# Linformer attention and a squared-ReLU FFN on one core: softmax sums of a whole batch in the free half of a PSUM pair, and the first batch's v ahead of the weights

## The chip, the core and the metric

The kernel runs on one core of a Trainium2 chip. The metric is device time in microseconds (us), lower is better. The core has TensorE (PE; its weight loads are shown as PEld), VectorE (DVE), ScalarE (ACT), GpSimd (POOL) and SyncE (SP). Transfers are issued from a queue of SP (plain copies and transposes) or of POOL (here all loads that turn float32 into bfloat16) and are carried out by 16 DMA engines. Matmul results go to PSUM, which has eight banks of 512 float32 per partition.

## What is computed

```python
k_proj = einsum('ks,bhsd->bhkd', E, k)          # B = 8, H = 8, S = 1024, D = 64; 64 projected keys
v_proj = einsum('ks,bhsd->bhkd', F, v)
scores = q @ k_proj.T / sqrt(D)
attn = exp(scores - max); attn = attn / (sum(attn) + 1e-9)
x = (attn @ v_proj) as (B*S, H*D)               # 8192 x 512
out = relu(x @ w_in) ** 2 @ w_out               # 512 -> 2048 -> 512
```

Inputs and output are float32; the kernel works in bfloat16 with float32 sums.

## The kernel before, in words

**Tiling.** A batch is 1024 tokens, cut into two chunks of 512 (`Chunk`). Attention of a batch (`Attention`) works on head pairs: `project` makes k and v projections of all heads with 16 matmuls into the two banks of one PSUM pair (k into rows 0 to 63 of bank 0, v into rows 64 to 127 of bank 1; the other halves of both banks are unused, L267 to L274). A DMA transpose makes `kT` from `kp` (L304), another makes `qT` from `Q_sb` (L331). `scores(pr)` multiplies them for one head pair (L363) and ScalarE takes the exponential into `expT`. `sums_spread(pr)` (L387) sums the exponentials of two head pairs with eight matmuls against a block of ones, each into 32 rows; ScalarE inverts the sums as exp(-ln) over 128 x 1024 (L397, L398), and eight copies on SP's queue spread them over the partitions as `rs` (L404). `values(pr)` (L407) multiplies the exponentials with v, and VectorE multiplies the result with `rs` into `xT` (L420).

**FFN.** Both layers use Strassen's seven products instead of eight, with pre-made sums of the weights (`w_in_sum`, `w_out_sum`), of `xT` (`sum_x`) and of `h` (`sum_h`). `Group` makes the first layer (L666), `second_spread` the second (L586). Batch 0 is an exception: its first layer runs as plain 512-column matmuls (`first_cold`, `first_plain`, L503), and `second_seven` (L563) does the second layer of its first chunk.

**Order.** TensorE's order is written out by hand. After the start, the generator `both()` (L863) takes one step after the other; a step is four matmuls of a first-layer product and four of a second-layer product, and a batch has 56 steps. `at` and `on` hang stages of attention on step numbers in `plan` (L753, L869), so that attention of the coming batches runs between the FFN products of earlier ones. The loop at L876 does so with t = 56 (b - 1) + 28. All other engines, and the queues of SP and POOL, are ordered by the framework's scheduler, which places each instruction by its own estimate of when its inputs are there; the order is fixed in the program, and each queue runs strictly in it.

**Buffers around the change.** From L824 on one PSUM pair serves all of attention (`att_psum`, L75), so each stage waits for the reader of the one before. `K_sb`, `Q_sb`, `V_sb`, `kp`, `kT` and `qT` have one buffer each, `vp` two, `expT` four, `rs` three, the output tile `o_sb` three. A load of the next `Q_sb` must wait until the DMA transpose has read the old one. `load_kv` and `load_q` are given a `behind` (L91): the load waits for a named instruction.

**Start of the run.** Transfers are issued in the order k (two heads as float32 on SP), k, q, F, k, q, v heads 0 to 3, then w_in piece 0, v heads 4 and 5, w_in piece 1, v heads 6 and 7, more w_in, the rest of q, and w_out (L102 to L146). `warm(n)` (L218) puts n matmuls on zeros between early stages. v's second half is projected in two pieces at steps 1 and 2 of `first_cold` (L778, L780), and `chunk_values` for heads 4 to 7 follows in two halves (L779, L781).

Of the kernel before, what the change touches and what calls it, by code (L numbers as in the profile page):

```python
# [9 lines left out]
P = 128  # L10
# [9 lines left out]
def kernel(  # L20
# [19 lines left out]
    NI = 8  # L40
# [61 lines left out]
    e_f32 = soft_pool.tile([KP, S], F32, tag="rs", name="e_f32")  # L102
    nc.sync.dma_start(e_f32[:], E[:])

    k_f32 = soft_pool.tile([P, 2, NI, D], F32, tag="rs", name="k_f32")
# [13 lines left out]
    V_PIECES = (slice(0, 4), slice(4, 6), slice(6, 8))  # L119
    load(V0[:, V_PIECES[0]], tokens(v, 0, h=V_PIECES[0]))  # L120
# [7 lines left out]
    W_IN_PIECES = ((0, 2), (2, 4), (4, 8), (8, 12), (12, 16))  # L128
# [100 lines left out]
    nc.vector.memset(kp[:], 0.0)  # L229
    kT = const_pool.tile([P, H, 2, KP], BF16, name="kT")  # L230
    VALUE_QUADS = ((LO, 0, 0, LO), (HI, 1, 1, HI), (HI, 0, 1, LO), (LO, 1, 0, HI))

    class Attention:
# [97 lines left out]
        def transpose_q_dma(self):  # L331
            nc.sync.dma_start_transpose(
                self.qT[:].rearrange("p h n t -> p (h n) t"), self.Q[:].rearrange("p h i d -> p (h i d)")
            )
# [22 lines left out]
        def inverse(self, ps):  # L357
            rs = soft_pool.tile([P, 2, TCH], F32, tag="rs", name="rs")
# [9 lines left out]
        def sums(self, pr):  # L368
# [8 lines left out]
            rs = [soft_pool.tile([P, 2, TCH], F32, tag="rs", name="rs") for _ in range(2)]  # L377
# [9 lines left out]
        def sums_spread(self, pr):  # L387

            ps = att_psum()
            for j in range(2):  # L390
                for o, par, a, r in VALUE_QUADS:
                    c = 32 * (2 * a + j)
                    nc.tensor.matmul(  # L393
                        ps[c:c + 32, par], lhsT=ones[r, 0:32], rhs=self.e[pr + j][r, a], start=True, stop=True
                    )
            inv = soft_pool.tile([P, 2, TCH], F32, tag="rs", name="inv")
            nc.scalar.activation(inv[:], ps[:], AF.Ln)  # L397
            nc.scalar.activation(inv[:], inv[:], AF.Exp, scale=-1.0)  # L398
            for j in range(2):
                rs = soft_pool.tile([P, 2, TCH], F32, tag="rs", name="rs")  # L400
                for a in range(2):
                    have = 32 * (2 * a + j)
                    for to in (64 * a, 64 * a + 32):
                        nc.sync.dma_start(rs[to:to + 32], inv[have:have + 32])  # L404
                self.rs[pr + j] = rs
# [316 lines left out]
    with tc.manual_schedule(engines={PE}):  # L722
# [152 lines left out]
        on(15, 1, "chunk_values", 1, 1)  # L875
        for b in range(B - 1):  # L876
            t = 56 * (b - 1) + 28
            if b:
                on(t + 1, b + 1, "scores", 3)
                on(t + 3, b + 1, "sums_spread", 2)  # L880
                on(t + 7, b + 1, "values", 0)
                on(t + 10, b + 1, "values", 1)
                on(t + 20, b + 1, "values", 2)
                on(t + 23, b + 1, "values", 3)
                at(t + 24, lambda b=b: chunk[b + 1, 0].sum_x())
            at(t + 51, lambda b=b: chunk[b + 1, 1].sum_x())
            if b + 2 < B:
                if b:
                    on(t + 11, b + 2, "load_q", lambda b=b: atts[b + 1].done)
                on(t + (26 if b else 32), b + 2, "transpose_q_dma")  # L890
                on(t + (28 if b else 36), b + 2, "project")
                on(t + (30 if b else 37), b + 2, "transpose_k_dma")
                if b + 3 < B:
                    at(t + (32 if b else 37), begin, b + 3)
                    on(t + (32 if b else 37), b + 3, "load_kv", lambda b=b: atts[b + 2].kT_done)
                on(t + (44 if b else 45), b + 2, "scores", 0)
                on(t + (47 if b else 48), b + 2, "scores", 1)
                on(t + (50 if b else 51), b + 2, "sums_spread", 0)
                on(t + (53 if b else 54), b + 2, "scores", 2)
# [34 lines left out]
```

## Time and profile before

| | |
|---|---|
| time, median of 3 runs | 475.4 us (475.11 to 475.48) |
| the profiled execution, its own time | 475.91 us, of which the span is 474.1 us |
| TensorE matmuls | 464.5 us, 98% of the span, 4136 instructions |
| VectorE | 348.1 us, 73% |
| ScalarE | 296.5 us, 63% |
| POOL | 34.3 us, 7% |
| granted TensorE clock | 1.0 |
| first-layer products L666, second-layer products L586 | 37.0% and 35.6% of the chain that ended last |
| Ln and Exp of the sums, L397 and L398 | 12 each, 1023 and 1062 ns |
| spreads `rs<-inv`, L404 | 96 on SP, 128 KB each, 2.3 us to landing (median) |
| loads of Q, K, V after the start | 1024 KB each as landed, medians 12.4, 10.2 and 14.8 us to landing |

How to read it: the span is the profiled time from the first to the last instruction. The "chain that ended last" follows the last instruction back through what released each step. A line of a timeline has start, duration, engine, line, operation, output and input, shapes and count; in brackets the idle time of that engine ahead of it and what ended it. Durations of single matmuls are modelled with their drain, so the step from one start to the next tells more than the duration. "To landing" is the time from the issue of a transfer to its completion.

### The profile page before, as it was taken

Reading aid. Unit: us, or ns where it says so; the run is one execution under the profiler, and the core shown is the slowest. Engines: PE = TensorE matmul, PEld = TensorE weight load, DVE = VectorE, ACT = ScalarE, POOL = GpSimd, SP = SyncE. Lnnn points to the kernel's source line nnn. Section 1 sums busy time; section 2 is a strip of 40 time slices with the busy share of each in tenths; the row PEclk is TensorE's granted clock in tenths of the full one; section 3 lists DMA queues with packets and bytes.
Section 4 is the critical chain, followed back from the end, with each engine's and each line's share of the span. In section 5 each row is a group of like instructions: output and inputs, shape, how many; then the busy total and the mean of one; then the engine's idle time right before and its main releaser. Section 6 shows DMA issues by size and latency. Waiting matters only on the chain.

```text
span 474.1 us, 10128 instructions
## 1 busy us (share of the span) xinstructions
PE 464.5 (98%) x4136; PEld 367.6 (78%) x4154; DVE 348.1 (73%) x593; ACT 296.5 (63%) x482; POOL 34.3 (7%) x47
## 2 busy tenths in 40 slices
PE   7899999999999999999999999999999999999996
PEld 3444587787888887887878888888878888888885
DVE  2468976776977779677895679777796778968571
ACT  2478676777556873687556775568736875565641
POOL 7430010100010000100001000100000000000000
PEclk9999999999999999999999999999999999999999
DMA  9999999795879568795987948796592054101012
GB/s 177 203 205 207 154 169 189 160 225 140 160 167 195 158 104 185 129 193 132 181 180 122 190 113 145 181 190 163 105 218 81 29 134 107 66 24 68 24 68 88
DMA packets 85231, 67.90 MB, mean 143 GB/s; under 512 B 34368, under 2 KB 81728, under 8 KB 85184
## 3 DMA queue, kind: packets, MB, share of 16 engines
q0 software_dynamic: 31696, 29.23, 40.3%
q1 hardware_dynamic: 53344, 37.89, 30.4%
q8 instruction: 32, 0.52, 0.4%
q10 hardware_dynamic: 144, 0.13, 0.1%
q14 instruction: 15, 0.12, 0.1%
HBM read 59.24 MB, written 16.78 MB: 160 GB/s over the span
## 4 chain that ended last, share of the span: by engine, by line
PE 93%; ACT 2%; DMA 2%; DVE 2%; issue 1%; ACTq 0%; DVEq 0%; POOLq 0%
PE ps_bank L666 37%; PE ps_second L586 36%; PE ps_bank L503 4%; PE ps_bank L563 3%; PE ps_att L271 3%; PE ps_att L340 2%; PE ps_second L563 2%; PE ps_att L416 2%; DMA K_sb<-in_k_dram 1%; PE ps_bank L315 1%; DVE xT L445 1%; PE ps_att L393 1%; DMA out_dram<-o_sb 1%; ACT h L496 1%; PE ps_att L350 0%
## 5 line engine op out<-in xcount | busy, mean ns | idle before, releaser
L156 DVE TENSOR_TENSOR h<-h 128x1024 bf16<-128x1024 bf16 (+1 forms) x170 | 105.4, 645 | 42.8 <-ACT h L676 38.7
L666 PE MATMUL ps_bank<-x_sum,w_in_sum 128*128 128x256 bf16 x672 | 101.1, 273 | 0.1
L666 PEld LDWEIGHTS <-w_in_sum 128*128 128x128 bf16 x896 | 85.5, 98 | 18.9 <-issue 6.3
L586 PEld LDWEIGHTS <-h 128*128 128x128 bf16 x896 | 87.6, 98 | 10.7
L680 DVE CUSTOM_DVE_ANT_0 h<-ps_bank,u 128x512 bf16<-128x512 f32 x112 | 73.8, 685 | 16.2 <-PE ps_bank L666 12.1
L558 ACT COPY u<-ps_bank 128x512 f32<-128x512 f32 x115 | 68.0, 591 | 24.9 <-PE ps_bank L666 23.6
L691 ACT COPY ps_bank<-ps_bank 128x512 f32<-128x512 f32 x56 | 32.0, 571 | 81.5 <-PE ps_bank L666 81.5
L676 ACT ACTIVATE h<-ps_bank 128x512 bf16<-128x512 f32 x112 | 67.9, 607 | 16.7 <-PE ps_bank L666 15.8
L666 PEld LDWEIGHTS <-w_in 128*128 128x128 bf16 x672 | 64.3, 98 | 14.5 <-issue 5.2
L586 PEld LDWEIGHTS <-s 128*128 128x128 bf16 x672 | 65.8, 98 | 7.6
L666 PE MATMUL ps_bank<-xT,w_in 128*128 128x256 bf16 x448 | 67.3, 273 | 0.3
L586 PE MATMUL ps_second<-w_out_sum,s 128*128 128x256 bf16 x448 | 67.2, 273 | 0.0
L586 PE MATMUL ps_second<-w_out_sum,h 128*128 128x256 bf16 x448 | 67.1, 273 | 0.0
L586 PE MATMUL ps_second<-w_out,h 128*128 128x256 bf16 x448 | 64.7, 272 | 0.0
L420 DVE TENSOR_TENSOR xT<-ps_att,rs 128x512 bf16<-128x512 f32 x48 | 30.9, 685 | 14.2 <-PE ps_att L416 14.2
L354 ACT ACTIVATE expT<-ps_att 128x1024 bf16<-128x1024 f32 x32 | 33.1, 1034 | 6.1 <-PE ps_att L340 4.4
L666 PE MATMUL ps_bank<-x_sum,w_in 128*128 128x256 bf16 x224 | 33.7, 273 | 0.3
L666 PE MATMUL ps_bank<-xT,w_in_sum 128*128 128x256 bf16 x224 | 33.6, 273 | 0.1
L586 PE MATMUL ps_second<-w_out,s 128*128 128x256 bf16 x224 | 33.6, 273 | 0.0
L156 DVE TENSOR_TENSOR o_sb<-ps_second,u 128x512 f32<-128x512 f32 x29 | 19.9, 685 | 18.7 <-PE ps_second L586 13.6
L503 PE MATMUL ps_bank<-xT,w_in 128*128 128x512 bf16 x124 | 29.7, 379 | 2.0 <-DVE xT L445 1.6
L156 DVE TENSOR_TENSOR s<-h 128x1024 bf16<-128x1024 bf16 x32 | 22.0, 691 | 4.5 <-PE ps_second L586 2.7
(97 smaller groups left out, 452.3 us busy)
## 6 DMA issues: line engine op xcount, KB each, us to landing
out_dram<-o_sb SPq DMA_DIRECT2D x63, 256.0 KB, 2.4
rs<-inv SPq DMA_DIRECT2D x96, 128.0 KB, 2.3
K_sb<-in_k_dram POOLq DMA_DIRECT2D x7, 1024.0 KB, 10.2
V_sb<-in_v_dram POOLq DMA_DIRECT2D x7, 1024.0 KB, 14.8
Q_sb<-in_q_dram POOLq DMA_DIRECT2D x6, 1024.0 KB, 12.4
w_out<-in_moe_w_out_dram POOLq DMA_DIRECT2D x4, 512.0 KB, 17.4
w_in<-in_moe_w_in_dram POOLq DMA_DIRECT2D x3, 512.0 KB, 14.5
Q_sb<-in_q_dram POOLq DMA_DIRECT2D x4, 256.0 KB, 10.8
```

The source lines that it names most:

```text
L156: return nc.vector.tensor_tensor(out=o, in0=x, in1=y, op=op)
L271: nc.tensor.matmul(ps[LO, 0], lhsT=ET[:, i, :], rhs=self.K[:, :, i, :], start=f, stop=l)
L354: self.done = nc.scalar.activation(e[:], ps[:], AF.Exp, scale=SCALE)
L420: self.done = nc.vector.tensor_tensor(out=self.xT[:, pr, :, par], in0=ps_x[par].rearrange("p (c t) -> p c t", c=2), in1=rs[:, par].rearran ...
L503: nc.tensor.matmul(ps[:], lhsT=w_in_blk(cb, fb), rhs=self.xT[:, cb, self.c].rearrange("p a t -> p (a t)"), start=(cb == 0), stop=(cb == NC ...
L558: nc.scalar.copy(u[:], ps)
L563: nc.tensor.matmul(ps[:, i * HM:(i + 1) * HM], lhsT=self.h_form(n, fb)[:, i * P:(i + 1) * P], rhs=w_out_form(n, fb), start=fresh and i == ...
L586: nc.tensor.matmul(ps[:, i * HM:(i + 1) * HM], lhsT=self.h_form(n, fb)[:, i * P:(i + 1) * P], rhs=w_out_form(n, fb), start=fresh and i == ...
L666: nc.tensor.matmul(ps[:, j * HC:(j + 1) * HC], lhsT=w_in_form(n, cb, 2 * self.g + j), rhs=self.chunk.x_form(n, cb), start=fresh and j == 0 ...
L676: nc.scalar.activation(self.out(kh, a), ps[:], AF.Relu)
L680: nc.vector._custom_dve(TENSOR_ADD_SAT, out=self.out(kh, a), in0=ps[:], in1=more[:], s0=3.0e38, s1=0.0)
L691: nc.scalar.copy(self.chain[:], self.first[:])
```

## The change

1. **Start.** v's second half goes as one load ahead of all weights; w_in's third piece is cut in two. `project_v` for heads 4 to 7 and `chunk_values` for them stand before the first projection, with five warming matmuls between; `kp` is cleared by ScalarE instead of VectorE; `chunk_values(1, 1)` moves from step 14 to 13.
2. **Sums.** `sums_all` sums all four head pairs with 16 matmuls into one 128 x 512 result: `pick[r, m]` has ones in eight of its 32 columns, so that pair m adds to eight rows of each 32-row block. From batch 3 on its matmuls stand behind those of `project` of the following batch, in the free halves of the same PSUM pair. Ln runs on each half (64 x 512), Exp once on 128 x 512. For batches 2 and 7 `sums_alone` does it in a pair of its own.
3. **Spreads.** `spread(pr)` copies eight rows eightfold into 64, four copies a head pair: pairs 0 and 1 from SP's queue, pairs 2 and 3 from POOL's. `rs` has two buffers now, `inv` one.
4. **Order.** `project`, loads, transposes, `scores`, `spread` and `values` get new steps. The transpose of the next Q is issued behind the last spread of pairs 0 and 1. `load_q` no longer waits for `values`, only for its buffer.

```diff
--- before.py
+++ after.py
@@ -99,10 +99,10 @@
         return t
 
 
-    e_f32 = soft_pool.tile([KP, S], F32, tag="rs", name="e_f32")
+    e_f32 = soft_pool.tile([KP, S], F32, tag="rs", bufs=2, name="e_f32")
     nc.sync.dma_start(e_f32[:], E[:])
 
-    k_f32 = soft_pool.tile([P, 2, NI, D], F32, tag="rs", name="k_f32")
+    k_f32 = soft_pool.tile([P, 2, NI, D], F32, tag="rs", bufs=2, name="k_f32")
     nc.sync.dma_start(k_f32[:], tokens(k, 0, h=slice(0, 2)))
 
     K0, Q0, V0 = (qkv_pool.tile([P, H, NI, D], BF16, name=n) for n in ("K_sb", "Q_sb", "V_sb"))
@@ -116,8 +116,8 @@
         if g == 0:
             make_identity(nc, ident[:])
             load(f_bf[:], F[:])
-    V_PIECES = (slice(0, 4), slice(4, 6), slice(6, 8))
-    load(V0[:, V_PIECES[0]], tokens(v, 0, h=V_PIECES[0]))
+    for h in half:
+        load(V0[:, h], tokens(v, 0, h=h))
     nc.scalar.preload_act_table_set("natural_log_exp_and_others")
     zeros = const_pool.tile([P, 512], BF16, name="zeros")
     nc.vector.memset(zeros[:], 0.0)
@@ -125,7 +125,7 @@
     nc.vector.memset(ones[:], 1.0)
 
 
-    W_IN_PIECES = ((0, 2), (2, 4), (4, 8), (8, 12), (12, 16))
+    W_IN_PIECES = ((0, 2), (2, 4), (4, 6), (6, 8), (8, 12), (12, 16))
     w_in_view = moe_w_in.rearrange("(cb p) f -> p cb f", p=P)
     w_out_view = moe_w_out.rearrange("(fb p) m -> p fb m", p=P)
     w_in_at, w_out_sb = {}, []
@@ -134,9 +134,7 @@
         load(t[:], w_in_view[:, :, lo * P:hi * P])
         for fb in range(lo, hi):
             w_in_at[fb] = (t, fb - lo)
-        if j < 2:
-            load(V0[:, V_PIECES[j + 1]], tokens(v, 0, h=V_PIECES[j + 1]))
-        if j == 2:
+        if j == 3:
             for g in range(2):
                 load(Q0[:, half[g], 4:8, :], tokens(q, 0, h=half[g], i=slice(4, 8)))
     fn = NFB // WP
@@ -226,8 +224,14 @@
 
 
     kp = const_pool.tile([P, H, 2, D], BF16, name="kp")
-    nc.vector.memset(kp[:], 0.0)
+    for h in half:
+        nc.scalar.copy(kp[:, h].rearrange("p h a d -> p (h a d)"), zeros[:])
     kT = const_pool.tile([P, H, 2, KP], BF16, name="kT")
+
+    pick = const_pool.tile([P, H // 2, 32], BF16, name="pick")
+    nc.scalar.copy(pick[:].rearrange("p m k -> p (m k)"), zeros[:, 0:P])
+    for m in range(H // 2):
+        nc.scalar.copy(pick[:, m, 8 * m:8 * m + 8], ones[:, 0:8])
     VALUE_QUADS = ((LO, 0, 0, LO), (HI, 1, 1, HI), (HI, 0, 1, LO), (LO, 1, 0, HI))
 
     class Attention:
@@ -264,14 +268,20 @@
             nc.scalar.copy(self.vp[HI], view)
             nc.vector.tensor_copy(self.vp[LO], view)
 
-        def project(self):
+        def project(self, sums=None):
             ps = att_psum()
             for i in range(NI):
                 f, l = i == 0, i == NI - 1
                 nc.tensor.matmul(ps[LO, 0], lhsT=ET[:, i, :], rhs=self.K[:, :, i, :], start=f, stop=l)
                 nc.tensor.matmul(ps[HI, 1], lhsT=FT[:, i, :], rhs=self.V[:, :, i, :], start=f, stop=l)
+            if sums:
+                sums.sums_all(ps)
+                sums.log(1)
             self.keep_k(ps[LO, 0], slice(0, H))
             self.keep_v(ps[HI, 1])
+            if sums:
+                sums.log(0)
+                sums.inverse_all()
 
         def project_k(self, g):
             ps = bank()
@@ -328,10 +338,11 @@
                     )
             nc.vector.tensor_copy(self.qT[:, 2 * pr:2 * pr + 2], ps[:])
 
-        def transpose_q_dma(self):
-            nc.sync.dma_start_transpose(
-                self.qT[:].rearrange("p h n t -> p (h n) t"), self.Q[:].rearrange("p h i d -> p (h i d)")
-            )
+        def transpose_q_dma(self, behind=None):
+            with tc.issue_after(atts[behind].spread_done.ins) if behind else nullcontext():
+                nc.sync.dma_start_transpose(
+                    self.qT[:].rearrange("p h n t -> p (h n) t"), self.Q[:].rearrange("p h i d -> p (h i d)")
+                )
 
 
         def scores_mm(self, ps, pr, n):
...
@@ -384,25 +395,39 @@
                     nc.vector.tensor_copy(rs[j][lack:lack + 32], rs[j][have:have + 32])
                 self.rs[pr + j] = rs[j]
 
-        def sums_spread(self, pr):
-
-            ps = att_psum()
-            for j in range(2):
+        def sums_all(self, ps=None):
+
+
+            ps = att_psum() if ps is None else ps
+            for m in range(H // 2):
                 for o, par, a, r in VALUE_QUADS:
-                    c = 32 * (2 * a + j)
+                    c = HI.start * (1 - par) + 32 * a
                     nc.tensor.matmul(
-                        ps[c:c + 32, par], lhsT=ones[r, 0:32], rhs=self.e[pr + j][r, a], start=True, stop=True
+                        ps[c:c + 32, par], lhsT=pick[r, m], rhs=self.e[m][r, a],
+                        start=m == 0, stop=m == H // 2 - 1, skip_group_check=True,
                     )
-            inv = soft_pool.tile([P, 2, TCH], F32, tag="rs", name="inv")
-            nc.scalar.activation(inv[:], ps[:], AF.Ln)
-            nc.scalar.activation(inv[:], inv[:], AF.Exp, scale=-1.0)
-            for j in range(2):
-                rs = soft_pool.tile([P, 2, TCH], F32, tag="rs", name="rs")
-                for a in range(2):
-                    have = 32 * (2 * a + j)
-                    for to in (64 * a, 64 * a + 32):
-                        nc.sync.dma_start(rs[to:to + 32], inv[have:have + 32])
-                self.rs[pr + j] = rs
+            self.inv = soft_pool.tile([P, TCH], F32, tag="inv", name="inv", bufs=1)
+            self.ps_sums = ps
+
+        def log(self, par):
+            rows = (HI, LO)[par]
+            nc.scalar.activation(self.inv[rows], self.ps_sums[rows, par], AF.Ln)
+
+        def inverse_all(self):
+            nc.scalar.activation(self.inv[:], self.inv[:], AF.Exp, scale=-1.0)
+
+        def spread(self, pr):
+            rs = soft_pool.tile([P, 2, TCH], F32, tag="rs", bufs=2, name="rs")
+            for o, par, a, r in VALUE_QUADS:
+                c = HI.start * (1 - par) + 32 * a + 8 * pr
+                self.spread_done = (nc.sync if pr < 2 else nc.gpsimd).dma_start(rs[o, par], self.inv[c:c + 8].unsqueeze(1).broadcast_to((8, 8, TCH)))
+            self.rs[pr] = rs
+
+        def sums_alone(self):
+            self.sums_all()
+            self.log(1)
+            self.log(0)
+            self.inverse_all()
 
         def values(self, pr, spare=False):
 
@@ -742,11 +767,14 @@
         warm(2)
         att.chunk_scores(0, 1)
         warm(2)
-        att.project_v(V_PIECES[0])
+        att.project_v(half[0])
         warm(1)
         att.chunk_sums(0, 1)
         att.chunk_values(0, 0)
+        warm(3)
+        att.project_v(half[1])
         warm(2)
+        att.chunk_values(0, 1)
 
         plan = {}
 
@@ -775,10 +803,6 @@
 
         begin(1)
         nxt = atts[1]
-        at(1, att.project_v, V_PIECES[1])
-        at(2, att.chunk_values, 0, 1, (0,))
-        at(2, att.project_v, V_PIECES[2])
-        at(3, att.chunk_values, 0, 1, (1,))
         at(3, nxt.load_kv)
         at(6, att.transpose_q_chunk, 1, Q0, 0)
         at(7, att.transpose_q_chunk, 1, Q0, 1)
@@ -788,8 +812,8 @@
         at(9, att.chunk_sums, 1, 0)
         at(10, att.chunk_sums, 1, 1)
         at(12, att.chunk_values, 1, 0)
-        at(14, att.chunk_values, 1, 1)
-        for n, step in enumerate((9, 17, 18)):
+        at(13, att.chunk_values, 1, 1)
+        for n, step in enumerate((9, 17, 18, 18)):
             at(step, sum_w_in, chunk[0, int(n > 0)], n)
         at(18, chunk[0, 0].sum_h, 0)
         at(20, chunk[0, 0].sum_h, 1)
@@ -873,30 +897,50 @@
         on(6, 1, "chunk_values", 1, 0)
         on(12, 1, "chunk_sums", 1, 1)
         on(15, 1, "chunk_values", 1, 1)
+        on(4, 2, "transpose_q_dma")
+        at(5, begin, 3)
+        on(5, 3, "load_q")
+        on(8, 2, "project")
+        on(9, 2, "transpose_k_dma")
+        on(10, 3, "load_kv", lambda: atts[2].kT_done)
+        for pr in range(4):
+            on((18, 20, 22, 24)[pr], 2, "scores", pr)
+            if pr < 2:
+                on(27, 2, "spread", pr)
+        plan[27].insert(0, lambda: atts[2].sums_alone())
+        on(42, 3, "project")
+        on(43, 3, "transpose_k_dma")
+        on(28, 3, "transpose_q_dma", 2)
+        at(32, begin, 4)
+        on(32, 4, "load_q")
+        on(44, 4, "load_kv")
         for b in range(B - 1):
             t = 56 * (b - 1) + 28
-            if b:
-                on(t + 1, b + 1, "scores", 3)
-                on(t + 3, b + 1, "sums_spread", 2)
-                on(t + 7, b + 1, "values", 0)
-                on(t + 10, b + 1, "values", 1)
-                on(t + 20, b + 1, "values", 2)
-                on(t + 23, b + 1, "values", 3)
-                at(t + 24, lambda b=b: chunk[b + 1, 0].sum_x())
             at(t + 51, lambda b=b: chunk[b + 1, 1].sum_x())
+            if not b:
+                continue
+            if b > 1:
+                if b + 2 < B:
+                    at(t - 10, lambda b=b: atts[b + 2].project(atts[b + 1]))
+                    on(t - 9, b + 2, "transpose_k_dma")
+                else:
+                    on(t - 10, b + 1, "sums_alone")
+                for pr in range(2):
+                    on(t - 9, b + 1, "spread", pr)
+                if b + 2 < B:
+                    on(t - 9, b + 2, "transpose_q_dma", b + 1)
+                    if b + 3 < B:
+                        at(t + 12, begin, b + 3)
+                        on(t + 18, b + 3, "load_kv", lambda b=b: atts[b + 1].done)
+                        on(t + 12, b + 3, "load_q")
+            for pr in range(4):
+                on(t + (9, 12, 19, 23)[pr] if b == 1 else t + (7, 11, 17, 21)[pr], b + 1, "values", pr)
+                if pr < 2:
+                    on(t + ((9, 12) if b == 1 else (7, 11))[pr], b + 1, "spread", pr + 2)
+            at(t + 24, lambda b=b: chunk[b + 1, 0].sum_x())
             if b + 2 < B:
-                if b:
-                    on(t + 11, b + 2, "load_q", lambda b=b: atts[b + 1].done)
-                on(t + (26 if b else 32), b + 2, "transpose_q_dma")
-                on(t + (28 if b else 36), b + 2, "project")
-                on(t + (30 if b else 37), b + 2, "transpose_k_dma")
-                if b + 3 < B:
-                    at(t + (32 if b else 37), begin, b + 3)
-                    on(t + (32 if b else 37), b + 3, "load_kv", lambda b=b: atts[b + 2].kT_done)
-                on(t + (44 if b else 45), b + 2, "scores", 0)
-                on(t + (47 if b else 48), b + 2, "scores", 1)
-                on(t + (50 if b else 51), b + 2, "sums_spread", 0)
-                on(t + (53 if b else 54), b + 2, "scores", 2)
+                for pr in range(4):
+                    on(t + (29, 36, 40, 44)[pr], b + 2, "scores", pr)
         steps = both()
         run(steps)
         assert not plan, plan
```

More of the change, by code (lines that the diff above doesn't have):

```diff
@@ L1 @@
-from contextlib import ExitStack
+from contextlib import ExitStack, nullcontext
 import concourse.bass as bass
@@ L376, in sums @@
                     )
-            rs = [soft_pool.tile([P, 2, TCH], F32, tag="rs", name="rs") for _ in range(2)]
+            rs = [soft_pool.tile([P, 2, TCH], F32, tag="rs", bufs=2, name="rs") for _ in range(2)]
             nc.scalar.activation(rs[1][:], ps[:], AF.Ln)
@@ L385, in sums @@
                 self.rs[pr + j] = rs[j]
[L387 to L390 removed]
+        def sums_all(self, ps=None):
+            ps = att_psum() if ps is None else ps
+            for m in range(H // 2):
                 for o, par, a, r in VALUE_QUADS:
[L392 removed]
+                    c = HI.start * (1 - par) + 32 * a
                     nc.tensor.matmul(
[L394 to L405 removed]
+                        ps[c:c + 32, par], lhsT=pick[r, m], rhs=self.e[m][r, a],
+                        start=m == 0, stop=m == H // 2 - 1, skip_group_check=True,
+                    )
+            self.inv = soft_pool.tile([P, TCH], F32, tag="inv", name="inv", bufs=1)
[6 more added lines that the diff above has]
+        def spread(self, pr):
+            rs = soft_pool.tile([P, 2, TCH], F32, tag="rs", bufs=2, name="rs")
+            for o, par, a, r in VALUE_QUADS:
[7 more added lines that the diff above has]
+            self.inverse_all()
         def values(self, pr, spare=False):
```

## Prediction, made before the changed kernel ran

> **What bounds the kernel now.** I read the page's busy shares and chain first, then TensorE's timeline at the start and in one batch, then the queues of GpSimd (POOL) and SyncE (SP) with the landings of their transfers.
>
> ```profile
> PE 464.5 (98%) x4136; PEld 367.6 (78%) x4154; DVE 348.1 (73%) x593; ACT 296.5 (63%) x482; POOL 34.3 (7%) x47
> ...
> PE 93%; ACT 2%; DMA 2%; DVE 2%; issue 1%; ACTq 0%; DVEq 0%; POOLq 0%
> ```
>
> TensorE is busy 98% of the span and 93% of the chain. So cheaper sums on ScalarE buy nothing by themselves; only TensorE's own work and its few waits count. TensorE's timeline at the start (start, us, line) has those waits:
>
> ```profile
> 18.72 0.38 PE L222 MATMUL ps_bank<-zeros 128*128 128x512 bf16 x1 [0.16 <-issue]
> 19.43 0.38 PE L503 MATMUL ps_bank<-xT,w_in 128*128 128x512 bf16 x1 [0.33 <-DVE xT L445]
> ...
> 25.09 2.95 PE L503 MATMUL ps_bank<-xT,w_in 128*128 128x512 bf16 x12 [0.26 <-DVE xT L445]
> ...
> 40.90 0.38 PE L503 MATMUL ps_bank<-xT,w_in 128*128 128x512 bf16 x1 [0.24 <-DVE xT L445]
> 41.50 13.32 PE L503 MATMUL ps_bank<-xT,w_in 128*128 128x512 bf16 x59 [0.22 <-DVE xT L445]
> ```
>
> The first projection waits for `xT`. From 41.5 it runs 59 matmuls back to back, 0.219 us each. In a steady batch nothing waits:
>
> ```profile
> 263.63 0.60 PE L586 MATMUL ps_second<-w_out,s 128*128 128x256 bf16 x4
> 264.16 0.41 PE L393 MATMUL ps_att<-expT,ones 64*32 64x512 bf16 x8
> 264.50 0.61 PE L666 MATMUL ps_bank<-x_sum,w_in_sum 128*128 128x256 bf16 x4
> ```
>
> Four 256-column matmuls take 0.437 us (starts 264.50 to 264.95), so the sums, inserted between 264.07 and 264.50, cost 0.44. A group of `values` costs 0.44 too (277.20 to 277.64), a pair of scores 0.44, a `project` 1.95. Per batch: 448 x 0.1094 + 4 x 0.44 + 2 x 0.44 + 4 x 0.44 + 1.95 = 55.4, and one batch takes 55.34 (a first projection starts at 188.66, its successor at 244.00). There is no stall to remove there.
>
> **The change, part by part.**
>
> *Start.* V's second half (512 KB as landed) now goes ahead of the first weights. V's first half lands at 15.9 (issued 5.77, 10.1 to land); 256 KB more take 1.3 us in this backlog (the next weight piece lands at 17.2), so V is whole at 18.4 and the weights come at 19.7 and 21.0. From 18.72: three warming matmuls to 19.4, `project_v` 1.0 (L290: 16.56 to 17.56) to 20.4, its copy 0.42 to 20.9, eight `values` 0.34 to 21.3; then the 16 first matmuls unbroken, 3.5 us, to 24.8, with `xT` ready ahead of them (two products of 0.65 each to 22.7). Before they end at 25.09 + 4 x 0.219 = 25.96: 1.15 gained. `values` of the second chunk moves one step up, and in VectorE's new order its `xT` stands before the first `h` sum (0.60): most of the two waits at 41 goes, 0.45. Together **-1.6**; at least -0.5 (the weights, now later, hold something), at most -2.4 (every wait listed up to 41.5, and the saved matmuls). The clearing of `kp` and the `pick` copies go to ScalarE, idle for 3.43 us before 5.45: nothing.
>
> *Sums on TensorE.* Before, the eight matmuls of a call use eight different 64x32 corners, and eight of 512 columns fit in 0.34 us. Now the four head pairs accumulate into the same four corners, so four rounds of 0.213 us follow each other: 0.85, plus about 0.13 for the change of shape straight behind `project` (L279 to L346 at 13.51: 0.99 for 0.85 of columns). That is 0.98 against 0.88, four times; alone (batches 2 and 7) 0.85 + 0.23 = 1.08, twice: **+0.8** in all. If the corners did not run side by side, 16 x 0.213 = 3.4 each: +15.
>
> *ScalarE and VectorE.* Two Ln and two Exp of 1.02 and 1.06 become three of 0.58 (row L264, 64x512). ScalarE is no bound (81.5 us of waits at L691 alone): nothing. The scores of batch 2 stand two steps apart, 2.2 us, with one exponential of 1.03 and two copies of 0.59: it just fits, 0 to +0.5; taken as 0.
>
> *Queues.* This part decides. In the changed program's order, POOL's queue holds batch b+3's Q load, and behind it the eight spreads of head pairs 2 and 3, which were on SP. That Q load waits for the transpose of the previous Q (one `Q_sb` buffer), and this transpose stands on SP behind the eight spreads of pairs 0 and 1. So it goes for batches 3, 4 and 5. Before, POOL's queue held only loads, and SP's the spreads and transposes:
>
> ```profile
> 251.72 0.87 POOL L89 DMA_DIRECT2D K_sb<-in_k_dram  x1 [23.49 <-PE ps_bank L666]
> 252.59 0.88 POOL L89 DMA_DIRECT2D V_sb<-in_v_dram  x1
> 282.41 0.88 POOL L89 DMA_DIRECT2D Q_sb<-in_q_dram  x1 [28.94 <-DVE xT L420]
> ```
>
> SP's timeline at the same place:
>
> ```profile
> 279.12 5.43 SPq L404 DMA_DIRECT2D rs<-inv  x8
> ...
> 295.24 3.97 SPq L332 DMA_TRANSPOSE qT<-Q_sb  x1
> ```
>
> Landings (last column, us after issue) of the Q load above, and then of the next K and V, issued at 306.18 and 307.04:
>
> ```profile
> Q_sb<-in_q_dram POOLq DMA_DIRECT2D x1, 1024.0 KB, 12.8
> ```
>
> ```profile
> K_sb<-in_k_dram POOLq DMA_DIRECT2D x1, 1024.0 KB, 10.2
> V_sb<-in_v_dram POOLq DMA_DIRECT2D x1, 1024.0 KB, 14.4
> ```
>
> V, issued 0.87 behind K, lands 5.1 behind it. All 21 loads of the first 60 us also land in their order of issue: a spread behind a load lands behind that load.
>
> Count from the end of `project` with sums (step t-10). Ln 0.58, two `kp` copies 0.68, `vp` 0.58 and 0.69, Ln and Exp 1.16 go to and fro between ScalarE and VectorE, with two L680 and one L558 in their queues (1.2 and 0.6): Exp ends at 6.2. Eight spreads on SP, 5.0: 11.2. Transpose, 5.7 to land: 16.9. Q load issued 17.0, landed 12.3 later (the five steady Q loads: 11.6 to 12.8): 29.3. The spreads behind it at 0.5 each (128 KB of F landed 0.5 behind Q at the start): the third at 30.8. But `values` of pair 2 stands 27 steps of 0.875 and two groups of 0.44 later, so VectorE wants that spread at 25.5. VectorE stands in its queue; behind the two L420 products (0.68 each) and a sum of 0.6, TensorE waits for the shared PSUM pair at `values` of pair 3, due at 28.6, until 32.9: **4.3** lost, three times.
>
> Batch 2: sums end, Exp at 2.0, spreads to 7.0, transpose to 12.7; POOL has three spreads of pair 2 out by then (0.8 each after the first `values`), so Q goes at 13.1 and lands at 25.4, the fourth spread at 25.9. VectorE wanted it at 22, TensorE wanted the L680 behind it at 23.4 and gets it at 27.3: **3.9**. Batches 6 and 7 have no Q load ahead; there ten steps cover the spreads (without that cover, 4 each more). The spreads left on SP land by 13.5, wanted at 15. SP's stores stand behind spreads and transpose, but held up to 10 us behind it before without a wait on TensorE. K and V, issued after `values` of pair 2, land within 15 and are wanted some 25 later. Sum 3 x 4.3 + 3.9 = **16.8**. With K's 10.2 in place of 12.3 it is 3 x 2.2 + 1.8 = 8.4; with the quickest such load (8.7, K at 58.72) 2.4; with no wait behind the load 0; with 12.8, 18.8. I take 12.3: same tensor, same place in the batch.
>
> [...]
>
> **Sum.** The profiled execution took 475.91 (span 474.1, 1.8 around it). 475.9 - 1.6 + 0.8 + 16.8 = 491.9; the median of the three runs is 0.5 lower than that execution: **491.4**.
>
> **Rivals.** *(A) Forecast*, Q takes 10 us or more: 482 to 495. Chance 0.58. *(B) Short load*: Q lands in 8 to 10, stalls of 0.3 to 2 each: 475.7 to 482. For it: the 8.7. Against: all five steady Q loads. 0.12. *(C) No stall, the other side*: the small spreads do not wait behind the load, or Q lands within 7.0 us of its issue (25.5 less 17.0 and 1.5; the point from which it decides). For it: VectorE's L420 never waited for a spread before. Against: then no spread stood behind a load. 475.4 - 1.6 + 0.8 = 474.6, from 473.8 to 475.7. 0.22. *(D) Worse*: POOL's spreads are late in batches 6 and 7 too, as VectorE crowds POOL, or the sums' corners run one by one (the change not doing what it says): 495 to 506. 0.08.
>
> **How the numbers follow.** A is likeliest: 491.4. A alone leaves out too much, so the range reaches through B to C's side: 474 to 495. About 0.2% (0.95 us) is what a measurement tells from no change: slower = A + B + D = 0.78; C splits into faster 0.14 and within 0.2% 0.08.
>
> **What would show it.** In the new trace: L420's successor waiting for a DMA of `rs`, four times, some 4 to 5 us each, near the batches' second half and none in the last two; Q landing in 11 to 13; the 16 sums taking 0.95 to 1.1; first matmuls of 512 columns ending by 25. A Q load under 8 us, or spreads landing before the load ahead of them, makes the forecast wrong.

## The result, and the profile after

| | before | changed |
|---|---|---|
| median, us | 475.4 (475.1 to 476.7) | 550.4 (546.1 to 551.1) |
| ratio | | 1.155, 95% interval 1.149 to 1.162 |
| span of the profiled execution, us | 474.1 | 548.9 |

The change makes the kernel 75 us slower, nearly five times the loss of 16 that was forecast. The page of the changed kernel has TensorE's share and granted clock, the chain that ended last, and the line of `values`:

```profile
PE 480.8 (88%) x4118; PEld 375.8 (68%) x4141; DVE 350.5 (64%) x595; ACT 286.0 (52%) x483; POOL 61.4 (11%) x95
...
PEclk9999999998599996999869999699996999999999
...
PE 62%; DMA 20%; SPq 7%; DVE 5%; ACT 3%; issue 2%; POOL 1%; DVEq 0%; POOLq 0%; ACTq 0%
...
L445 DVE TENSOR_TENSOR xT<-ps_att,rs 128x512 bf16<-128x512 f32 x48 | 32.0, 688 | 82.0 <-DMA rs<-inv 66.3
```

TensorE fell from 98% to 88% of the span, the granted clock dips five times, and transfers and SP's queue now hold 27% of the chain, where they held 2%. VectorE waited 66.3 us for `rs` at L445; its predecessor L420 had not waited for a spread once.

One steady batch shows the chain of causes. TensorE's timeline where batch 3's `values` are due (start, us, line, operation; in brackets the idle time ahead):

```profile
201.90 0.60 PE L611 MATMUL ps_second<-w_out_sum,h 128*128 128x256 bf16 x4
212.50 0.64 PE L441 MATMUL ps_att<-expT,vp 64*64 64x512 bf16 x4 [10.01 <-DVE xT L445]
213.07 1.04 PE L691 MATMUL ps_bank<-xT,w_in 128*128 128x256 bf16 x4
213.90 1.06 PE L611 MATMUL ps_second<-w_out,s 128*128 128x256 bf16 x4
214.76 1.06 PE L691 MATMUL ps_bank<-x_sum,w_in_sum 128*128 128x256 bf16 x4
```

The wait is 10 us. After it, four matmuls take 0.85 us from start to start instead of 0.44: the clock granted between 212.5 and 218.0 was 0.51. What VectorE waited for, and the queues of SP and POOL ahead of it:

```profile
194.71 0.69 DVE L445 TENSOR_TENSOR xT<-ps_att,rs 128x512 bf16<-128x512 f32 x1 [1.94 <-DMA rs<-inv]
...
210.56 0.69 DVE L445 TENSOR_TENSOR xT<-ps_att,rs 128x512 bf16<-128x512 f32 x1 [9.44 <-DMA rs<-inv]
```

```profile
178.65 10.45 SPq L423 DMA_DIRECT2D rs<-inv  x8
189.20 7.09 SPq L343 DMA_TRANSPOSE qT<-Q_sb  x1
```

```profile
198.93 0.88 POOL L89 DMA_DIRECT2D Q_sb<-in_q_dram  x1 [61.24 <-DMA qT<-Q_sb]
200.12 3.94 POOL L423 DMA_DIRECT2D rs<-inv  x7 [0.32 <-ACT u L583]
```

Eight spreads hold SP's queue for 10.45 us; before, eight took 4.96 to 5.43. The transpose behind them takes 7.09 instead of 4.0, so the Q load goes 9.2 us later than the prediction had it (26.2 us behind the sums instead of 17.0), and POOL's spreads behind it.

The waits of over 0.5 us on TensorE, batch by batch, beside the forecast:

| batch whose `values` wait | 2 | 3 | 4 | 5 | 6 | 7 |
|---|---|---|---|---|---|---|
| idle, us | 2.9 + 14.2 | 1.0 + 10.0 | 3.7 + 8.2 | 1.7 + 10.4 | 0.8 + 7.5 | 0 |
| lost to the half clock after them | 2.8 | 2.7 | 4.4 | 1.7 | 3.0 | 0 |
| forecast | 3.9 | 4.3 | 4.3 | 4.3 | 0 | 0 |

The half clock's loss is half of the time that TensorE worked while 0.5 was granted. From the start of the second layer to the end, the span grew by 75.7 us (495.2 against 419.5): 60.5 idle, 14.6 half clock, 0.6 of sums (six times 0.97 to 0.98 against 0.88). Nothing of size is left over.

### The profile page after: what moved, and what is told of

Same layout as the page of the kernel before. It is cut to its first block, busy times and chain, and to the rows that moved or that the text cites. A ratio compares the mean times of both kernels' runs of the same rounds, so it can differ in the third digit from the quotient of the medians.

```text
span 548.9 us, 10159 instructions
## 1 busy us (share of the span) xinstructions
PE 480.8 (88%) x4118; PEld 375.8 (68%) x4141; DVE 350.5 (64%) x595; ACT 286.0 (52%) x483; POOL 61.4 (11%) x95
## 4 chain that ended last, share of the span: by engine, by line
PE 62%; DMA 20%; SPq 7%; DVE 5%; ACT 3%; issue 2%; POOL 1%; DVEq 0%; POOLq 0%; ACTq 0%
PE ps_bank L691 22%; PE ps_second L611 21%; DMA rs<-inv 15%; SPq L423 7%; PE ps_bank L528 5%; PE ps_bank L588 3%; DMA qT<-Q_sb 3%; PE ps_att L351 2%; PE ps_att L275 2%; PE ps_second L588 2%; DVE xT L445 1%; PE ps_att L405 1%; DMA out_dram<-o_sb 1%; DVE h L705 1%; PE ps_att L441 1%
## 5 line engine op out<-in xcount | busy, mean ns | idle before, releaser
L691 PE MATMUL ps_bank<-x_sum,w_in_sum 128*128 128x256 bf16 x672 | 103.9, 278 | 21.8 <-DVE h L705 21.5
L691 PEld LDWEIGHTS <-w_in_sum 128*128 128x128 bf16 x896 | 88.0, 99 | 40.8 <-issue 25.6
L445 DVE TENSOR_TENSOR xT<-ps_att,rs 128x512 bf16<-128x512 f32 x48 | 32.0, 688 | 82.0 <-DMA rs<-inv 66.3
L611 PEld LDWEIGHTS <-s 128*128 128x128 bf16 x672 | 68.9, 103 | 10.8
L691 PE MATMUL ps_bank<-xT,w_in 128*128 128x256 bf16 x448 | 69.1, 278 | 0.1
L423 POOL DMA_DIRECT2D rs<-inv x48 | 27.0, 578 | 147.3 <-DMA out_dram<-o_sb 56.5
L441 PE MATMUL ps_att<-expT,vp 64*64 64x512 bf16 x96 | 11.2, 458 | 36.1 <-DVE xT L445 36.1
L611 PE MATMUL ps_second<-w_out,s 128*128 128x256 bf16 x224 | 39.2, 305 | 0.0
L691 PE MATMUL ps_bank<-x_sum,w_in 128*128 128x256 bf16 x224 | 35.9, 286 | 0.3
L89 POOL DMA_DIRECT2D Q_sb<-in_q_dram x12 | 10.2, 851 | 218.5 <-DMA out_dram<-o_sb 110.0
## 6 DMA issues: line engine op xcount, KB each, us to landing
K_sb<-in_k_dram POOLq DMA_DIRECT2D x7, 1024.0 KB, 10.5
```

The source lines that it names most:

```text
L423: self.spread_done = (nc.sync if pr < 2 else nc.gpsimd).dma_start(rs[o, par], self.inv[c:c + 8].unsqueeze(1).broadcast_to((8, 8, TCH)))
L445: self.done = nc.vector.tensor_tensor(out=self.xT[:, pr, :, par], in0=ps_x[par].rearrange("p (c t) -> p c t", c=2), in1=rs[:, par].rearran ...
L611: nc.tensor.matmul(ps[:, i * HM:(i + 1) * HM], lhsT=self.h_form(n, fb)[:, i * P:(i + 1) * P], rhs=w_out_form(n, fb), start=fresh and i == ...
L691: nc.tensor.matmul(ps[:, j * HC:(j + 1) * HC], lhsT=w_in_form(n, cb, 2 * self.g + j), rhs=self.chunk.x_form(n, cb), start=fresh and j == 0 ...
```

## The experiments

Each time stands beside runs of the kernel before on the same chip. Three theories: **Q**, that of the prediction, the Q load ahead of POOL's spreads; **N**, the new form of the spread is slow on SP's queue; **C**, a transpose and spreads in flight together slow each other.

**1. The Q load behind POOL's spreads.**

```diff
-        on(32, 4, "load_q")
+        on(48, 4, "load_q", lambda: atts[2].done)
...
-                        on(t + 12, b + 3, "load_q")
+                        on(t + 18, b + 3, "load_q", lambda b=b: atts[b + 1].done)
```

> The changed kernel with batch b+3's Q load issued behind the eight spreads of pairs 2 and 3 instead of ahead of them. Theory Q (that of the prediction: the load ahead of the spreads makes the stall): the stalls of 8.2 to 14.2 us in batches 2 to 5 go, what is left is the 1 to 4 us that each batch waits for the spreads on SP's queue; 485 to 495 us. Theory N (each spread of eight source rows takes 1.3 us on SP's queue instead of 0.63, and everything behind is late): the Q load no longer matters, the same 485 to 495. Theory C (spreads and the transpose of Q in flight at the same time slow each other, as in batch 6, where no Q load stands ahead and TensorE still waits 7.5 us, the transpose taking 15.5 us instead of 4.0): POOL's spreads now start straight into the transpose in every batch; the stalls stay at 7 to 14 us in batches 2 to 6 and the transposes take 10 us or more; 520 to 545.

Measured 540.6 us (ratio 1.137, 1.129 to 1.144). Without a load ahead of them the spreads of batches 3 to 6 are as late: waits of 8.2 to 9.1 us each. SP's timeline in batch 3, and the landing of POOL's spreads (last column, us after issue):

```profile
186.05 15.28 SPq L343 DMA_TRANSPOSE qT<-Q_sb  x1
```

```profile
rs<-inv POOLq DMA_DIRECT2D x48, 128.0 KB, 14.9
```

The transpose takes 15.28 us. So theory Q alone does not set the loss: take the load away and the spreads come as late, beside a slow transpose.

**2. The same without the transposes of Q from batch 3 on.** The scores of batches 3 to 7 use batch 2's `qT`; the order of everything else in the queues stays.

```diff
         def transpose_q_dma(self, behind=None):
+            if self.b > 2:
+                return
...
-            self.qT = qt_pool.tile([P, H, NT, P], BF16, name="qT")
+            self.qT = qt_pool.tile([P, H, NT, P], BF16, name="qT") if b <= 2 else atts[2].qT
```

> The version with the Q load behind POOL's spreads (540.6 us), and in it the transposes of Q left out from batch 3 on: scores of batches 3 to 7 use batch 2's qT. All spreads, all loads and every other transfer stay. Theory C (a transpose and POOL's spreads in flight together slow each other; there the transposes took 15.1 us): without the transposes POOL's spreads land in time, the stalls of 8 to 9 us in batches 3 to 6 go, what stays is the 1 to 4 us of SP's late spreads: 480 to 495 us. If POOL's spreads are late for another reason: 530 to 540, the same stalls.

Measured 487.8 us (1.024, 1.020 to 1.029): 53 us of the 65 above the kernel before are gone, though all spreads, SP's eight in 10.5 us or more too, and all loads are still there.

```profile
rs<-inv POOLq DMA_DIRECT2D x48, 128.0 KB, 7.3
```

POOL's spreads land in 7.3 us instead of 14.9. Theory C holds: with the Q load out of the way, the collision is 53 of the 65 us. Left are waits of 3.5 and 2.0 us in batch 2 and one of 0.9.

The DMA view shows the collision itself. The first fence is the changed kernel from 401 to 417 us, where batch 6 has a transpose and POOL's spreads in flight and no Q load anywhere; the second a transpose alone, in experiment 3, from 167 to 172 (busy share in tenths, and GB/s, in 40 slices):

```profile
DMA  5999352299799991999943904989999969493999
GB/s 90 131 142 42 36 44 39 42 192 113 143 164 88 60 49 15 88 36 25 24 34 3 19 0 70 82 108 289 289 287 314 205 53 250 89 143 84 343 154 167
```

```profile
DMA  0000000000299999999999999999999999999999
GB/s 0 0 0 0 0 0 0 0 0 0 59 246 295 293 283 293 291 289 289 293 291 283 285 289 287 285 279 281 285 283 279 264 266 258 250 279 274 254 215 252
```

Alone, the transpose moves some 285 GB/s and is done in 4.1 us. Beside spreads both kinds together move 0 to 88 GB/s for 5.6 us on end (14 slices). In nine of these slices the engines count as 90% busy or more, in the others as partly idle: here the two do not share the rate, they lose it. Without the transpose, in experiment 2, batch 6 has no wait over 0.5 us.

**3. The transpose ahead of the spreads.**

```diff
-        on(28, 3, "transpose_q_dma", 2)
+        on(28, 3, "transpose_q_dma")
...
-                    on(t - 9, b + 2, "transpose_q_dma", b + 1)
+                    on(t - 9, b + 2, "transpose_q_dma")
```

> The changed kernel without the rule that the transpose of the next Q stands behind the spreads of pairs 0 and 1: on SP's queue it now stands ahead of them, and of the transpose of k, so that it meets no spread, and the Q load behind it, still ahead of POOL's spreads in the queue, is issued some 20 us earlier. Theory Q and theory C: no long stall in any batch, the transposes take about 4 us; 475 to 480. Theory N: the eight spreads on SP still take 10.5 us, the second of them is 1 to 4 us late in each batch (1.0 to 3.7 in the changed kernel), six batches: 480 to 490. If POOL's spreads are late by themselves (9.6 us to landing in the changed kernel), stalls of 5 us or more stay in batches 2 to 7: above 500.

Measured 500.8 us (1.052, 1.046 to 1.057), above the 480 to 490 of theory N and in the "above 500" that was written for spreads late in every batch, which is not what happened. In batches 3 to 7 the transposes take 4.0 to 4.1 us and the waits are 0.8 to 2.0: there the forecast holds. The Q load is still ahead of the spreads in POOL's queue, but goes out 15 us before them (174.96, the first spread 190.21), so this does not test theory Q. What I missed is batch 2, where the transpose of batch 3's Q meets the loads of batch 3's K and V (issued at 89.3 and 90.2, landed at 103.2 and 109.9):

```profile
100.08 10.73 SPq L343 DMA_TRANSPOSE qT<-Q_sb  x1
110.90 0.53 SPq L605 DMA_DIRECT2D out_dram<-o_sb  x1
111.53 9.02 SPq L423 DMA_DIRECT2D rs<-inv  x8
```

Slowed to 10.73 us, it now holds up the spreads behind it, and TensorE waits 10.3 us, and 3.2 later for `kT`. So a transpose beside loads was slow as well, 10.73 us against 4.0 to 4.1.

**4 and 5. All spreads on one queue.** In line L423, `nc.sync` for all (4), and `nc.gpsimd` for all (5).

> The changed kernel with all sixteen spreads of a batch on SP's queue, none on POOL's; the transpose of Q stands between the first eight and the last eight. Theory Q: no spread stands behind a load, so the long stalls go; 480 to 490. Theory N: the last eight take another 10.5 us at 1.3 us each, behind the transpose: the pair 2 spreads land some 5 to 8 us late in batches 2 to 6; 515 to 535. Theory C: the transpose and the first spreads of the same queue overlap only at their ends, so the transposes take 4 to 7 us, not 12 to 15.

> The changed kernel with all sixteen spreads of a batch on POOL's queue, none on SP's; the transpose of Q then stands ahead of them in time, with the Q load behind it and ahead of the spreads in POOL's queue. Theory N (slow is the form on SP's queue, eight engines) and theory C (the transpose meets no spread): no stall over 2 us in batches 3 to 7, transposes of 4.1 us there; 475 to 485 us, below the 500.8 of the version with half of the spreads on SP. Theory Q: the first spreads now stand right behind the Q load, issued some 3 us ahead of them; they land 10 us late in batches 3 to 5; 505 to 520.

Measured 543.2 us on SP (1.142, 1.138 to 1.146), far above theory Q's 480 to 490 and somewhat above N's 515 to 535; waits of 9.1 to 9.2 us in batches 3 to 5, transposes of 6.7 to 8.8, where theory C had 4 to 7. On POOL 501.7 (1.055, 1.051 to 1.059), above the 475 to 485 of theories N and C. With no spread left on SP the transposes run ahead of the spreads, as in experiment 3, and that of batch 3's Q meets the loads again: 10.24 us. In batch 2 the Q load behind it, and the spreads behind that, are late:

```profile
114.41 0.87 POOL L89 DMA_DIRECT2D Q_sb<-in_q_dram  x1 [23.83 <-DMA qT<-Q_sb]
115.27 3.94 POOL L423 DMA_DIRECT2D rs<-inv  x7
```

TensorE waits 11.2 us there, and 3.0 later for `kT`: here theory Q's path does act. In batches 3 to 7 no other wait is over 1.9. The Q load goes early there; in batch 3 the spreads, issued 2.3 us behind it, land 9.8 us after their issue, which is in time. Theory Q would have had 505 to 520.

**6 to 8. The form, in the kernel before.** The queue and the number and bytes of the copies stay; the source rows of a spread change (n stands for 8, 16 and 32). With the new form the scheduler also placed ScalarE's second Ln ahead of an `h`, and one store between two groups of four spreads. SP, POOL, ScalarE and VectorE run the same order in all three kernels, so these differ from each other in the rows alone, but from the kernel before in this order too.

```diff
-                    for to in (64 * a, 64 * a + 32):
-                        nc.sync.dma_start(rs[to:to + 32], inv[have:have + 32])
+                    for par in range(2):
+                        nc.sync.dma_start(rs[64 * a:64 * a + 64, par],
+                            inv[have:have + n, par].unsqueeze(1).broadcast_to((n, 64 // n, TCH)))
```

> The kernel before, in its own order, with only the form of the spreads changed to that of the changed kernel: eight source rows, each copied eightfold, into 64 x 512, as many copies of as many bytes (96 of 128 KB). Theory N: each takes 1.3 us on SP's queue instead of 0.63, eight of them 10.5 us; half of the 16 engines carry it. The second and fourth pair's land about when VectorE wants them: 475.5 to 482 us. If the 1.3 us came from the other transfers of the changed kernel and not from the form: 0.63 to 0.7 each, and 475.4 us.

> The kernel before with its spreads as copies of sixteen source rows, each fourfold, into 64 x 512: the same number of copies, bytes and packet size as with eight rows eightfold (619.0 us), only more rows in the outer dimension. Theory N in the form that the outer dimension sets how many of the 16 engines carry a copy: sixteen packets in flight again, 0.6 to 0.7 us each on SP's queue; 475 to 477 us. If the packets of 2 KB or the repeated source rows are what is slow: still over 1.3 us each, over 560 us.

> The kernel before with its spreads as copies of thirty-two source rows, each twice, into 64 x 512: 128 KB a copy as ever, packets of 2 KB as with eight and sixteen rows. Eight rows gave 619.0 us with at most eight spread packets in flight, sixteen gave 518.9 with up to twenty. If what sixteen rows still lose comes from the packets (half the bytes each, yet often as long: 0.29 us): some 515 to 520 again. If it comes from reading few rows many times over: near 475.2 to 480. Either way up to sixteen or more in flight.

| source rows, packet | time, us | ratio | eight on SP's queue | drained in | GB/s | most spread packets in flight |
|---|---|---|---|---|---|---|
| 32, 4 KB (before) | 475.2 | 1 | 5.0 | 5.2 | 202 | 18 |
| 32, 2 KB | 486.8 | 1.024 (1.021 to 1.027) | 5.1 | 5.7 | 184 | 21 |
| 16, 2 KB | 518.9 | 1.091 (1.088 to 1.095) | 6.5 | 8.9 | 118 | 20 |
| 8, 2 KB | 619.0 | 1.301 (1.296 to 1.305) | 14.2 | 18.0 | 58 | 8 (9 or 10 for 0.5% of the time) |

"Drained" is the time from the first to the last packet of a batch's first eight spreads, from the packets' records; GB/s is 1 MiB by that time. My expectations were far off twice: 619 instead of 475.5 to 482, and 518.9, between the two theories' values; 486.8 is above the 475.2 to 480 that few rows alone would have given. From 32 rows to eight the time grows by 132 us; the 11.6 us between the kernel before and 32 rows hold the changed order too and are not priced apart. I had looked only for spreads that come late to VectorE. The wait sits elsewhere, in ScalarE's rows of the kernel with eight source rows:

```profile
187.64 0.64 ACT L676 ACTIVATE h<-ps_bank 128x512 bf16<-128x512 f32 x1
201.48 1.02 ACT L397 ACTIVATE inv<-ps_att 128x1024 f32<-128x1024 f32 x1 [13.20 <-DMA out_dram<-o_sb]
```

The Ln of the second sums takes a buffer of the three-buffer ring that `inv` and `rs` share, and gets it when the first eight spreads have read it; the profile names the transfer that came last, a store, but its wait shrinks with the drain: 13.2, 4.0, at most 1.5, and 0.2 us in the rows of the table from the bottom up. ScalarE stands in its queue, and TensorE behind it.

The series shows two parts in theory N. Packets: with eight rows hardly ever more than eight run at once, with sixteen up to twenty, so with eight rows at most about half of the 16 engines carry a spread at any moment; from 181 to 196 us of that kernel, where a batch's first eight spreads run, the mean busy share of the engines is 3 to 5 tenths from the first packet on. Why eight rows run fewer packets is not shown. Rows: from sixteen to thirty-two about as many packets are in flight (20 and 21), and the rate still rises by half, from 118 to 184 GB/s. From sixteen to eight both change, and what each is worth there is not shown.

In the changed kernel the same form drains in 11.9 to 17 us, and in 9.7 to 10.4 in batches 3 to 5 of experiment 3. In both, successive copies read different rows, while here two in a row read the same, which may be why it is quicker there; that was not tried by itself. The 1.3 us a copy on the queue is an average too: single copies took 0.60 to 0.65 us in batch 3 of experiment 3, and 0.6 to 2.1 in that of the changed kernel, the later ones longer.

**9. The mechanism on record, with the time that it assumed.** The kernel leaves out half of SP's spreads; ScalarE fills their places with zeros, and a few stores and transposes of `k` move in SP's queue.

```diff
+                if pr < 2 and (o, par) in ((HI, 0), (LO, 1)):
+                    nc.scalar.copy(rs[o, par], zeros[o])
+                    continue
```

> The changed kernel with half of the copies on SP's queue left out (rs of pairs 0 and 1 is half filled with zeros by ScalarE): four spreads of 1.3 us stand ahead of the transpose, 5.2 us, which is what the prediction gave to eight. So the mechanism on record runs with the time that it assumed: Q load ahead of POOL's spreads, no more delay ahead of it. Theory Q with the prediction's own numbers: stalls of about 4 us in batches 2 to 5, none in 6 and 7: 491 us. With theory C beside it: the transpose meets POOL's spreads in batch 6 still, 8 to 10 us there, and the half clock after each stall of over 3 us costs 2 to 3 us more: 500 to 510.

Measured 523.8 us (1.100, 1.096 to 1.104), above the 500 to 510 of theory C. In batch 3:

```profile
171.85 5.13 SPq L426 DMA_DIRECT2D rs<-inv  x4
177.02 9.34 SPq L343 DMA_TRANSPOSE qT<-Q_sb  x1
```

```profile
188.99 0.88 POOL L89 DMA_DIRECT2D Q_sb<-in_q_dram  x1 [52.50 <-DMA qT<-Q_sb]
190.13 3.94 POOL L426 DMA_DIRECT2D rs<-inv  x7 [0.26 <-DVE h L154]
```

The spreads take the 5.1 us that the prediction gave them, and the transpose still takes 9.34 on the queue and 12.0 until the Q load goes, not 5.7: it starts at 177.02, and the packets of the spreads ahead of it move until 184.3. With that the waits are 9.2, 7.5, 7.6 and 9.3 us in batches 2 to 5, about twice the forecast. Batch 6 has only 0.7 and 0.8, so my 8 to 10 us for it were wrong: its transpose takes 11.55 us, but POOL's spreads land in 7.9 instead of 13.9 (median), perhaps because fewer are in flight; that was not tried.

**10. No spreads at all.** `spread` hands out a tile of ones, nothing is issued. With the spreads goes the rule that puts the transpose behind them, so the transposes run earlier.

> The changed kernel with all spreads left out: values are multiplied with a tile of ones, the sums, their Ln and Exp and all else stay. It prices everything of the change except the spreads and what they meet. Prediction's sum for that: -1.6 + 0.8, 474.4; by the trace of the changed kernel -0.9 + 0.6, 474.9. If the new order holds a wait of its own (scores, project, the loads), over 478.

Measured 474.9 us (0.9986, 0.9965 to 1.0007). TensorE is busy 99% of the span, no wait after the start exceeds 0.5 us, and the transpose of batch 3's Q takes 10.71 us beside loads without anyone waiting for it. So, within 2 us, all that the change costs comes from the spreads and what they meet.

**11. The start alone, on the kernel before** (the diff's parts on `V0`, `W_IN_PIECES`, `kp`, `project_v`, `chunk_values`, `sum_w_in`).

> The kernel before with the start alone taken from the change (v whole ahead of the weights, the third weight piece cut in two, projection and values of heads 4 to 7 ahead of the first layer, kp cleared by ScalarE, the last values of the start one step earlier), its steady part as it was. The prediction's step was -1.6 us (473.8). The trace of the changed kernel has the second layer starting at 53.75 instead of 54.66, so -0.9: 474.3.

Measured 474.5 us, before 476.6 on this chip: 0.9956 (0.9942 to 0.9971), some 2 us faster than the kernel before, and the fastest whole version here. My -0.9 was read badly: executions differ by 2 us in when `project_v` first runs (16.03 to 18.00 over thirteen profiles, whatever the start), and the changed kernel's was a late one. Counted from that event to the first matmul of the second layer, the old start takes 38.10 us in all four of its profiles and the new one 36.17 or 36.18 in all nine: -1.9.

## Why the prediction was wrong, step by step

- **Sign, and the path in batches 2 to 5: right.** `rs` became what VectorE waits for at L445, in four batches behind a Q load, none in batch 7. In batch 3 the load went 9.2 us later than forecast and landed 2.1 quicker; the prediction's own sum then gives 4.3 + 9.2 - 2.1 = 11.4, beside a wait of 10.0. What failed are the terms ahead of that load, and that a second path, the collision, was as long without it (experiment 1).
- **"Eight spreads on SP, 5.0": the step that failed first.** 0.63 each came from L404, a copy of 32 rows. Eight copies of eight rows took 10.5, 1.3 each on average, and the kernel before with that form is 30% slower, 27% slower than with 32 rows in the same order. It was a duration from the row of another form, taken without bounds.
- **"Transpose, 5.7 to land": failed, and weighs more.** The row was of a transpose that ran alone. Beside spreads it takes 7.1 to 15.5 us; moving it away took 50 us off (experiment 3), while the spreads ahead of it cut to 5.1 us took 27 (experiment 9). The prediction moved it next to spreads on two queues and did not ask what it meets.
- **"There ten steps cover the spreads" (batch 6): failed** for the same collision, 0.8 + 7.5 us. Rival D had the effect with another cause, VectorE crowding POOL, which no trace shows; batch 7, without a transpose, had none.
- **What a stall costs: a term was missing.** Each wait was priced as its length. The half clock behind the waits added 14.6 us in all.
- **Q load of 12.3 us: too long.** It landed in 10.2 in batch 3, median 10.0. By the prediction's sum that spared 2 us a batch. (The loads issued in the first 60 us are 25 in the profile, not 21; they do land in their order.)
- **Start, -1.6: right**, measured -1.9; only the way was different (the first matmuls ended at 25.9, not by 25, in an execution that began 1.0 late).
- **Sums, +0.8: nearly right.** The sixteen matmuls take 0.97 behind `project` (forecast 0.98) and 0.98 alone (1.08), in all 0.6. From the second layer's start to the end, the version without spreads is 1.3 us longer than the kernel before; the other 0.8 were not located.
- **Rival C's sum**, everything but the queues, 474.6, is what experiment 10 measured, 474.9. Its condition, no stall, was the one that failed.

## What to carry to other kernels

A copy's duration belongs to its form: eight copies of 128 KB held SP's queue for 5.0 us with 32 source rows (the kernel before) and for 14.2 with eight (experiment 6). Before a row of the trace is used for a new copy, compare how many source rows it reads and how many packets it can have in flight, not its bytes. A step that is moved must be looked at for what it meets in flight, above all a DMA transpose, whose 4 us alone became up to 15.7 beside spreads or loads. And a wait of TensorE can cost more than its length: behind the longest wait of each batch, 7.5 to 14.2 us, the matmuls of the changed kernel ran at half clock for another 3.4 to 6.1 us.

## What the runs showed of the hardware that was not expected

- A DMA transpose of 1 MB took 4.0 us alone, 10.7 beside loads and up to 15.7 beside spreads, and beside spreads the two together fell below 50 GB/s at times, where the transpose alone moves some 285. Why is open; what was shown is that it goes when one of the two is taken away or moved. Whether spreads of 32 rows slow a transpose as much no run shows: none was in flight beside one of Q.
- The same eight-row copy issued by POOL appears as packets of 4 KB with 17 to 23 in flight at most (experiments 5 and 2, and the changed kernel), on SP as packets of 2 KB with eight. So copies on POOL's queue are not held to eight packets together; whether a single one is was not looked at.
- The clock fell to half for 3.4 to 17 us at a time, always in steps of 3.41 us, behind waits or within them. The shortest of these waits were 1.95 us (experiment 2, ended at 139.8 us) and 2.15 (eight rows, at 241.1); after 3.34 us in experiment 4 (at 150.2) and 2.98 with 32 rows it did not fall. The length of a wait alone does not decide it.
